# Attention and two feed-forward layers on one core: seven block products in place of eight for three groups of down products of the first layer, three streamed blocks a pair, and first tiles' up products in two parts

## The chip, the cores and the metric

One core of a Trainium2 chip runs the whole program. The metric is the device time of one launch in microseconds, as the median of the runs. The engines are named as the profile names them: PE (TensorE matmul; PEld is its weight load), DVE (VectorE), ACT (ScalarE), POOL (GpSimd) and SP (SyncE, which here only issues transfers).

## The reference

Windowed attention, then a gated feed-forward layer (FFN1), then a second feed-forward layer (FFN2), on 2304 tokens of width 512, all in fp32.

```python
def reference(q, k, v, moe_*, moe2_*):
    attn = softmax(mask(q @ k.T / 8)) @ v            # 4 batches, 8 heads, 576 positions, width 64;
                                                     # each position sees at most 32 others
    x = attn.transpose(0, 2, 1, 3).reshape(2304, 512)
    g = x @ w_gate                                   # 512 -> 1536
    x = (silu(g) * (x @ w_val)) @ w_out              # 1536 -> 512
    h = x @ w_in                                     # 512 -> 2048
    return (h - tanh(h)) @ w_out2                    # 2048 -> 512
```

## The kernel before

**Numbers.** Every operand of a large product is kept as two float32r parts, a high and a low one, and a product of two operands is three matmuls (high·high, high·low, low·high; `PASSES`). The high part is made by a copy on ACT, the low part by a subtraction on DVE (`split_w`, `split_x`, `split_y`). Weights come as 64-bit words and are turned into fp32 on ACT and DVE (`convert`).

**Tiles.** The 2304 tokens are six tiles of 384 (`TT`). The hidden width is cut in blocks of 128, twelve in FFN1 (`k` = 0 to 11). The outer loop of FFN1 goes over groups of hidden blocks, `GROUPS1 = [1, 1, 2, 2, 2, 2, 2]`, so that groups begin at k = 0, 1, 2, 4, 6, 8 and 10. Inside a group the kernel goes over three pairs of tiles (`PAIRS`). For each it makes the *up* products (x times a gate and a value block, tile by tile of 384 columns), then the gating (`times_gate`, `times_val`: Silu on ACT, a multiplication on DVE), the split in two parts (`split_y`), and the *down* products (`ffn1_out`: w_out times y). The down results of a group are copied from PSUM to an `acc` buffer and added to sums in DRAM: the first group stores them (SP), later groups issue an accumulating transfer on POOL (`sum<-acc`), and the last group (k = 10) adds them on chip.

**Seven for eight.** From k = 2 on (`JOIN`), a group has two hidden blocks and a pair has two tiles, and each up product of 2 x 2 blocks (two hidden blocks, two tiles, two halves of the contraction) is made by seven block products (Strassen's scheme in Winograd's form) in place of eight: `seven_up`. It needs sums of weight blocks (`sums_w`) and sums of x blocks (`sums_x`): seven x blocks for each pair (B11, B21, B22, T1 to T4). Three PSUM banks carry a running value: ACT copies a bank's content into the next one (`seed`, the order names it `ps<-ps`), ACT keeps one (`keep`), and two additions on DVE end it. Of the seven x blocks, five stay in SBUF; the other two (T3 and T4) are stored to DRAM when they are made (`spill`, `part<-x`) and loaded again for each pair and group (`parts_of`, `x<-part`), unless the pair before in the program was the same one.

**Order.** Nothing runs in the order in which it is written: every piece of work is a task for a planner (`Plan`) with an engine, a duration, a priority (small first; `when` is a clock of PE work), what it depends on, and the buffers that it needs from rings of fixed sizes (`SLOTS`: 8 PSUM banks `ps`, 4 `acc`, 6 `y`, 6 `t`, 12 + 6 `x`, 10 + 1 `wc`). The planner plays the tasks through once while the program is built. What comes out is a fixed list of instructions for each engine, and each engine runs its list strictly in turn. SP's list holds the transfers of weights (`st<-w`), of attention's inputs (`q`, `v`) and of x blocks. The attention is mixed with the first up products in the first 130 us: its tasks make x piece by piece, heads 0 to 3 in the first of a tile's two x buffers and heads 4 to 7 in the second. A plain up product (`plain_up`, 12 matmuls) waits until both are complete.

## Time and profile before

| | |
|---|---|
| median of 3 runs | 894.3 us (893.83 to 896.32) |
| the profiled execution's own time | 895.31 us |
| its span, first to last instruction | 893.3 us |
| PE, PEld, DVE, ACT, POOL busy in the span | 98%, 93%, 74%, 63%, 11% |
| mean DMA rate | 214 GB/s |

Busy time is the union of an engine's instructions; PE's matmuls overlap, so that their starts tell its rate and not their lengths. A share over the whole span mixes stages: attention with the first groups to about 130 us, FFN1 to about 520 us, FFN2 to the end.

### The profile page before, as it was taken

The numbers are of one execution on the slowest core, as the hardware profiler recorded it, in microseconds if no ns is written. First come the engines' busy times: TensorE is split into PE (matmuls) and PEld (weight loads), VectorE is DVE, ScalarE is ACT, GpSimd is POOL, SyncE is SP. The second block draws the span as 40 slices with busy tenths as digits, with TensorE's granted clock in tenths as the row PEclk, the third lists the DMA queues.
The fourth block names the chain that finished last, engine by engine and source line by source line (L and its number), as shares of the span: only waits on it lengthen the run. The fifth ranks groups of instructions, "written<-read, shape, count | busy, mean of one in ns | idle before, by whom it ended". The sixth has DMA issues, their size and how long they took to land.

```text
span 893.3 us, 15217 instructions
## 1 busy us (share of the span) xinstructions
PE 878.7 (98%) x5310; PEld 829.5 (93%) x5310; DVE 657.6 (74%) x1577; ACT 565.8 (63%) x1467; POOL 94.3 (11%) x122
## 2 busy tenths in 40 slices
PE   7999999999999999999999999999999999999997
PEld 5899999999999999999999998898989989898995
DVE  6899989975645645644757999988887778765575
ACT  6798866756556655655656787765666656555431
POOL 2332220000000000000000000011110111110100
PEclk9899999999999999999999999999999999999999
DMA  9998736996775775686782568889988896968995
GB/s 281 288 293 263 241 114 157 325 299 136 197 184 106 200 189 107 179 210 142 215 266 89 222 227 314 247 211 273 230 212 210 203 252 162 232 127 209 250 286 211
DMA packets 48518, 191.17 MB, mean 214 GB/s; under 512 B 5552, under 2 KB 10672, under 8 KB 48432
## 3 DMA queue, kind: packets, MB, share of 16 engines
q1 hardware_dynamic: 38928, 138.20, 45.2%
q0 software_dynamic: 9504, 51.91, 31.6%
q8 instruction: 44, 0.72, 0.3%
q14 instruction: 42, 0.34, 0.1%
HBM read 114.59 MB, written 75.50 MB: 213 GB/s over the span
## 4 chain that ended last, share of the span: by engine, by line
PE 93%; DVE 3%; DMA 2%; ACT 1%; issue 0%; POOL 0%; SPq 0%; POOLq 0%
PE ps L467 44%; PE ps L667 22%; PE ps L647 16%; PE ps L455 5%; PE ps L371 2%; PE ps L425 2%; DMA q<-qk 2%; PE ps L396 1%; DVE x L439 1%; ACT e L382 1%; DMA mask<-masks 1%; DVE e L376 0%; DVE wc L278 0%; DVE u L301 0%; POOL e L390 0%
## 5 line engine op out<-in xcount | busy, mean ns | idle before, releaser
L467 PE MATMUL ps<-x,wc 128*128 128x384 f32 x2268 | 417.1, 337 | 0.0
L467 PEld LDWEIGHTS ps<-x,wc 128*128 128x128 f32 x2268 | 398.8, 188 | 5.2 <-issue 0.3
L667 PE MATMUL ps<-wc,y 128*128 128x512 f32 (+1 forms) x870 | 208.2, 391 | 0.9 <-DVE t L579 0.9
L612 ACT ACTIVATE acc<-ps 128x384 f32<-128x384 f32 (+1 forms) x246 | 127.4, 528 | 106.3 <-PE ps L667 55.4
L667 PEld LDWEIGHTS ps<-wc,y 128*128 128x128 f32 x870 | 161.8, 188 | 32.6 <-DVE t L579 1.3
L647 PE MATMUL ps<-y,wc 128*128 128x384 f32 x864 | 164.5, 337 | 0.0
L647 PEld LDWEIGHTS ps<-y,wc 128*128 128x128 f32 x864 | 150.9, 188 | 0.5 <-DVE acc L608 0.2
L633 POOL DMA_DIRECT2D sum<-acc x66 | 58.4, 884 | 667.5 <-ACT acc L612 308.4
L531 ACT ACTIVATE y<-t 128x384 fp32r<-128x384 f32 x168 | 86.8, 519 | 37.1 <-DVE t L560 25.1
L534 DVE TENSOR_TENSOR y<-t,y 128x384 fp32r<-128x384 f32 x168 | 92.3, 554 | 10.7 <-ACT y L531 9.9
L278 DVE TENSOR_TENSOR wc<-u,wc 128x512 fp32r<-128x512 f32 x104 | 70.7, 693 | 31.5 <-ACT wc L275 30.9
L275 ACT ACTIVATE wc<-u 128x512 fp32r<-128x512 f32 x104 | 64.9, 630 | 35.8 <-PE ps L467 19.7
L560 DVE SCALAR_TENSOR_TENSOR t<-t,ps 128x384 f32<-128x384 f32 x57 | 31.4, 552 | 64.0 <-PE ps L467 37.3
L478 ACT ACTIVATE ps<-ps 128x384 f32<-128x384 f32 x108 | 51.4, 477 | 26.8 <-PE ps L467 25.3
L576 DVE SCALAR_TENSOR_TENSOR t<-t 128x384 f32<-128x384 f32 x96 | 52.9, 555 | 13.3 <-ACT t L573 13.0
L507 DVE TENSOR_TENSOR ps<-ps,t 128x384 f32<-128x384 f32 x54 | 30.6, 566 | 39.2 <-PE ps L467 38.7
L382 ACT ACTIVATE e<-e,nm 128x96 f32<-128x96 f32 x144 | 52.0, 367 | 10.2 <-DVE nm L376 10.0
L573 ACT ACTIVATE t<-ps 128x384 f32<-128x384 f32 x72 | 35.0, 486 | 30.5 <-DVE ps L507 18.6
L455 PE MATMUL ps<-x,wc 128*128 128x384 f32 x288 | 53.5, 338 | 0.0
L455 PEld LDWEIGHTS ps<-x,wc 128*128 128x128 f32 x288 | 49.6, 188 | 0.2
L293 ACT ACTIVATE u<-st 128x512 f32<-128x512 f32 x68 | 45.1, 666 | 6.3 <-DVE wc L278 5.1
L301 DVE SCALAR_TENSOR_TENSOR u<-st,u 128x512 uint32<-128x512 uint32 x68 | 47.4, 697 | 0.8
(61 smaller groups left out, 795.4 us busy)
## 6 DMA issues: line engine op xcount, KB each, us to landing
sum<-acc POOLq DMA_DIRECT2D x66, 768.0 KB, 7.9
x<-part SPq DMA_DIRECT2D x60, 768.0 KB, 6.8
st<-w SPq DMA_DIRECT2D x68, 512.0 KB, 5.6
q<-qk SPq DMA_DIRECT2D x48, 304.0 KB, 6.8
sum<-acc SPq DMA_DIRECT2D x12, 768.0 KB, 5.8
part<-x SPq DMA_DIRECT2D x12, 768.0 KB, 4.4
acc<-sum SPq DMA_DIRECT2D x12, 768.0 KB, 8.1
v<-vt SPq DMA_DIRECT2D x48, 144.0 KB, 6.5
```

The costliest lines, as they stand in the source:

```text
L275: nc.scalar.activation(out=w()[:, 0, :], in_=u(), func=AF.Copy)
L278: nc.vector.tensor_tensor(out=w()[:, 1, :], in0=u(), in1=w()[:, 0, :].bitcast(F32), op=ALU.subtract)
L382: nc.scalar.activation(out=e()[:, i, :], in_=e()[:, i, :], func=AF.Exp, scale=-1.0, bias=nm()[:, i:i + 1], accum_out=sm()[:, i:i + 1])
L455: nc.tensor.matmul(ps()[:, :TT], lhsT=w()[:, a, kc * P:(kc + 1) * P], rhs=xt[kc // 2]()[:, bb, kc % 2, :], start=(n == 0), stop=(n == 3 * ...
L467: nc.tensor.matmul(ps()[:, :TT], lhsT=w()[:, i, c:c + P], rhs=b()[:, j, k, :], start=(start and n == 0), stop=(n == 5), skip_group_check=True)
L531: nc.scalar.activation(out=y()[:, 0, :], in_=s(), func=AF.Copy)
L534: nc.vector.tensor_tensor(out=y()[:, 1, :], in0=s(), in1=y()[:, 0, :].bitcast(F32), op=ALU.subtract)
L576: nc.vector.scalar_tensor_tensor(out=sq(), in0=sq(), scalar=E0 / E1, in1=sq(), op0=ALU.add, op1=ALU.mult)
L612: nc.scalar.activation(out=o, in_=ps()[:, :c1 - c0], func=AF.Copy)
L633: nc.gpsimd.dma_start(out=keep, in_=at(), accum_op=ALU.add)
L647: nc.tensor.matmul(ps()[:, :TT], lhsT=w[2][0]()[:, a, m * P:(m + 1) * P], rhs=y[0]()[:, bb, :], start=(start and n == 0), stop=(n == 3 * l ...
L667: nc.tensor.matmul(ps()[:, :c1 - c0], lhsT=y[0]()[:, a, s * P:(s + 1) * P], rhs=w[1][0]()[:, bb, c0:c1], start=(n == 0), stop=(n == 3 * le ...
```

## The change

1. In the groups k = 4, 6 and 8 (`SEVEN_DOWN`, all three pairs) the down products of two hidden blocks and two tiles are also made by seven block products for eight (`seven_out`, called in place of `ffn1_out`). They need sums of w_out blocks (`sums_out`, in two buffers `wm`), sums of the gated values (`sums_y`: four subtractions on DVE, and three splits more, in three buffers `ym`), and the seeding between PSUM banks that `seven_up` has.
2. While a pair's x blocks come from the attention (FFN1), four of the seven stay in SBUF and three (T2, T3, T4) go to DRAM and are loaded again. The first use at k = 2 takes them from the buffers in which they were made, without a load. For pair 1 these buffers are of a ring of their own (`xt`), whose room goes to `ym` and `wm` after k = 2 and then, after the last of them, to three more `x` buffers. FFN2 keeps five and streams two, as before.
3. For tiles 0 and 1 in the first group (`APART`), an up product is two tasks of six matmuls. The first needs only heads 0 to 3.

```diff
+Y_SOON, DELAY_7D = 30.0, 9.0
+APART = {(1, 0, 0), (1, 0, 1)}
...
-SLOTS = {"ps": (8, 0), "x": (2 * NT, 6), "acc": (4, 0), "wc": (10, 1), "y": (6, 0), "t": (6, 0), "st": (2, 0), "u": (4, 0), 
+SLOTS = {"ps": (8,), "x": (2 * NT, 3, 0, 0, 3), "xt": (0, 0, 3), "acc": (4,), "wc": (10, 1), "y": (6,), "t": (6,), "st": (2,), "u": (4,),
...
+         "q": (6,), "v": (7,), "e": (6,), "at": (4,), "nm": (8,), "sm": (8,), "ym": (0, 0, 0, 3), "wm": (0, 0, 0, 2)}
+HOMES = ("main", "late", "first", "mid", "last")
+SEVEN_DOWN = {(k, p) for k in (4, 6, 8) for p in range(3)}
...
+    def sums_out(c1, c2, prio):
...
+            tt(out=u2()[:, hi], in0=u1()[:, hi], in1=u2()[:, hi], op=ALU.add)
+            tt(out=u1()[:, hi], in0=u1()[:, lo], in1=u1()[:, hi], op=ALU.subtract)
+            tt(out=u1()[:, lo], in0=u2()[:, hi], in1=u1()[:, lo], op=ALU.subtract)
+            tt(out=u2()[:, lo], in0=u2()[:, lo], in1=u1()[:, lo], op=ALU.subtract)
+
+        a = plan.add("DVE", 1.2, prio, combine, [d1, d2], [u1, u2], port=True)
+        return split_w(u1, [a], prio, new_wm()), split_w(u2, [a], prio, new_wm())
...
-            a = plan.add("PE", MM * 12, prio, lambda wb=wb, ps=ps, xt=x[t]: up(wb, xt, ps), x_done[t] + [done],
-                         [wb, ps] + x[t])
+            ps, a = new_ps(), None
+            for chunks in ((range(KC // 2), range(KC // 2, KC)) if apart else (range(KC),)):
+                need = [d for h in range(2) if KC // 2 * h in chunks for d in x_done[t][h]]
+                a = plan.add("PE", MM * 3 * len(chunks), prio,
+                             lambda wb=wb, ps=ps, xt=x[t], chunks=chunks: up(wb, xt, ps, chunks), need + [done, a],
+                             [wb, ps] + x[t])
...
+    def sums_y(s11, s12, s21, s22, prio):
+
+        b11, b22, b21 = (split_y(*s, prio) for s in (s11, s22, s21))
...
+        t1 = step(s11, s12, s11, [b11[1], s12[1]])
+        y1 = split_y(s11[0], t1, prio, new_ym())
+        t3 = step(s12, s22, s12, [t1, s22[1]])
+        t2 = step(s22, s22, s11, [t3, b22[1]])
+        y2 = split_y(s22[0], t2, prio, new_ym())
+        y3 = split_y(s12[0], t3, prio, new_ym())
+        t4 = step(s21, s21, s22, [t2, b21[1]])
+        return b11, b21, b22, y1, y2, y3, split_y(s21[0], t4, prio)
...
+    def seven_out(ws, sums_o, blocks, tiles, prio):
...
+        for lo, hi in ((0, 2), (1, 3)):
+            pa, pb, pe, e = new_ps(), new_ps(), new_ps(), new_t()
...
+            p1 = pe_task(pa, wa, lo, B11, True, [], [pb, pe])
+            p5 = pe_task(pe, w41, hi, T1, True, [], [pa, pb])
+            sb = plan.add("ACT", 0.39, soon, sow(pb, pa), [p1], [pa, pb], lat=QUICK)
+            ke = plan.add("ACT", 0.39, soon, keep, [p5], [pe, e], lat=QUICK)
+            c11 = pe_task(pa, wb, lo, B21, False, [sb])
+            p6 = pe_task(pb, w23, lo, T2, False, [sb])
+            sc = plan.add("ACT", 0.39, soon, sow(pe, pb), [p6, ke], [pb, pe], lat=QUICK)
+            p3 = pe_task(pb, w41, lo, B22, False, [sc])
+            p7 = pe_task(pe, w23, hi, T3, False, [sc])
+            puts[0].append(plan.add("ACT", 0.39, prio, copy(at1, pa, lo), [c11], [pa, at1]))
+            puts[1].append(plan.add("DVE", 0.48, soon, add(at2, pb, lo), [p3, ke], [pb, e, at2], lat=QUICK))
+            c22 = plan.add("DVE", 0.48, soon, add(at2, pe, hi), [p7, ke], [pe, e, at2], lat=QUICK)
+            puts[1].append(c22)
+            c21 = pe_task(pe, wb, hi, T4, False, [c22])
+            puts[0].append(plan.add("ACT", 0.39, prio, copy(at1, pe, hi), [c21], [pe, at1]))
...
-    def spill(p, parts, prio):
-
-        seven_x[p], spilled[p] = parts[:5], []
-        for o, done in parts[5:]:
+    def spill(p, parts, kept, prio):
+
+        seven_x[p], spilled[p] = parts[:kept], []
+        for o, done in parts[kept:]:
...
+        if p in fresh:
+            fresh.remove(p)
+        elif not again or p not in fetched_x:
...
+                streamed.append(plan.add("NONE", 0.0, prio, lambda: None, [begun] + streamed[-1:], [o]))
+                fetched_x[p].append((o, plan.add("DMA", ISSUE, prio, load, [done, streamed[-1]], [o], lat=SLACK, work=2.15)))
...
+                    if p in down7:
+                        blocks = sums_y(ys[tiles[0]][0], ys[tiles[1]][0], ys[tiles[0]][1], ys[tiles[1]][1], when + 0.02 - Y_SOON)
+                        seven_out(ws, sums_o, blocks, tiles, when + DELAY_7D)
```

The built programs show where the planner now puts the work. Over the whole program PE has 54 matmuls of 384 columns fewer (down products in FFN1: 864 before; 432 plain and 378 in sevens now). DVE has 36 subtractions of `sums_y`, 27 splits into `ym`, 36 additions into `acc`, 12 sums of 256 columns and 6 splits of 512 columns more. ACT has 36 seeds, 18 keeps, 27 splits into `ym` and 6 into `wm` more, and 36 copies into `acc` fewer. SP has 3 stores and 3 loads of x blocks more.

**First place, PE near the start.** The rows of PE before, from the scores of one attention unit (`ps<-q`) on; transposes are `ps<-ident,e`, mixing `ps<-at,v`. `x_276` holds heads 0 to 3 of tile 0, `x_390` heads 4 to 7; `wc_471` and `wc_557` are the gate and value weights of block 0.

```order
L371 MATMUL ps_484<-q_281 128x96 x3
L396 MATMUL ps_508<-ident,e_422 96x128 x3
L371 MATMUL ps_518<-q_329 128x96 x3
L396 MATMUL ps_529<-ident,e_451 96x128 x3
L425 MATMUL ps_540<-at_473,v_270 64x64 x6
L425 MATMUL ps_540<-at_522,v_320 64x64 x6
L371 MATMUL ps_564<-q_363 128x96 x3
L371 MATMUL ps_582<-q_416 128x96 x3
L396 MATMUL ps_606<-ident,e_513 96x128 x3
L371 MATMUL ps_613<-q_438 128x96 x3
L455 MATMUL ps_630<-x_276,wc_471 128x384 x6
L455 MATMUL ps_630<-x_390,wc_471 128x384 x6
```

The same place with the change; everything ahead of it on PE and DVE stands as before.

```order
L395 MATMUL ps_484<-q_281 128x96 x3
L479 MATMUL ps_507<-x_276,wc_471 128x384 x6
L420 MATMUL ps_522<-ident,e_422 96x128 x3
L420 MATMUL ps_530<-ident,e_451 96x128 x3
L395 MATMUL ps_541<-q_329 128x96 x3
L395 MATMUL ps_549<-q_363 128x96 x3
L449 MATMUL ps_566<-at_473,v_270 64x64 x6
L449 MATMUL ps_566<-at_547,v_320 64x64 x6
L395 MATMUL ps_592<-q_416 128x96 x3
L420 MATMUL ps_604<-ident,e_516 96x128 x3
L395 MATMUL ps_610<-q_438 128x96 x3
L479 MATMUL ps_628<-x_276,wc_557 128x384 x6
```

Six matmuls of the first up product stand right behind the scores of `q_281`, ten rows earlier than before, and six of the value product take the place of the second half.

**Second place, PE in the group k = 4.** Before, one tile's down products: four PSUM banks, six matmuls each, in one piece.

```order
L647 MATMUL ps_3607<-y_3462,wc_3330 128x384 x3
L647 MATMUL ps_3607<-y_3577,wc_3558 128x384 x3
L647 MATMUL ps_3619<-y_3462,wc_3330 128x384 x3
L647 MATMUL ps_3619<-y_3577,wc_3558 128x384 x3
L647 MATMUL ps_3630<-y_3462,wc_3330 128x384 x3
L647 MATMUL ps_3630<-y_3577,wc_3558 128x384 x3
L647 MATMUL ps_3638<-y_3462,wc_3330 128x384 x3
L647 MATMUL ps_3638<-y_3577,wc_3558 128x384 x3
```

With the change, a part of a pair's down products (`y`, `ym` against `wc`, `wm`), three matmuls to a block product, between up products (`x`). `ps_4173`, `ps_4186` and `ps_4195` are the three banks of one half; the products into them wait for a seed (ACT) or an addition (DVE) in between.

```order
L490 MATMUL ps_4173<-y_3944,wc_3328 128x384 x3
L490 MATMUL ps_4119<-x_394,wc_3971 128x384 x6
L490 MATMUL ps_4110<-x_3708,wc_3979 128x384 x6
L490 MATMUL ps_4195<-ym_4007,wm_3629 128x384 x3
L490 MATMUL ps_4173<-y_4036,wc_3562 128x384 x3
L490 MATMUL ps_4186<-ym_4082,wm_3618 128x384 x3
L490 MATMUL ps_4214<-y_3944,wc_3328 128x384 x3
L490 MATMUL ps_4110<-x_3749,wc_3884 128x384 x6
L490 MATMUL ps_4186<-y_4033,wm_3629 128x384 x3
L490 MATMUL ps_4195<-ym_4072,wm_3618 128x384 x3
L490 MATMUL ps_4243<-ym_4007,wm_3629 128x384 x3
L490 MATMUL ps_4214<-y_4036,wc_3562 128x384 x3
```

Between the first product into `ps_4173` and the second stand 15 other matmuls; between the two into `ps_4186` stand 9.

**Third place, SP in the groups k = 4 and 6.** Before, each switch of pair loads two x blocks, mixed with weight loads.

```order
L710 DMA x_3391<-part 128x1536
L290 DMA st_3401<-w 128x512
L290 DMA st_3492<-w 128x512
L710 DMA x_3521<-part 128x1536
L290 DMA st_3542<-w 128x512
L710 DMA x_3616<-part 128x1536
L290 DMA st_3626<-w 128x512
L710 DMA x_3736<-part 128x1536
```

With the change, each loads three (`x_3481`, `x_3517`, `x_3552` for one pair, `x_3662`, `x_3708`, `x_3749` for the next).

```order
L298 DMA st_3397<-w 128x512
L814 DMA x_3481<-part 128x1536
L298 DMA st_3490<-w 128x512
L814 DMA x_3517<-part 128x1536
L814 DMA x_3552<-part 128x1536
L814 DMA x_3662<-part 128x1536
L298 DMA st_3692<-w 128x512
L814 DMA x_3708<-part 128x1536
L298 DMA st_3734<-w 128x512
L814 DMA x_3749<-part 128x1536
```

Three buffers take the streamed blocks in turn, so a block's load can start when PE has read the block of the pair before for the last time. Counted in PE's list between that last read and the first read of the new block, over the 21 loads from k = 4 to the first pair of k = 10, there stand 72 to 93 matmuls; before the change at least 114.

## Rows read from the trace of the kernel before

**Rows 1.** The page: busy time of the engines, and the chain that ended last by engine.

```profile
span 893.3 us, 15217 instructions
PE 878.7 (98%) x5310; PEld 829.5 (93%) x5310; DVE 657.6 (74%) x1577; ACT 565.8 (63%) x1467; POOL 94.3 (11%) x122
PE 93%; DVE 3%; DMA 2%; ACT 1%; issue 0%; POOL 0%; SPq 0%; POOLq 0%
```

**Rows 2.** Stretches: length, busy us (instructions) of each engine, clock, DMA share, GB/s.

```profile
247.00:316.00 69.00, 69.00 (x398) 69.00 (x397) 37.41 (x72) 40.20 (x83) 5.47 (x6) 1.00 0.65 160
316.00:385.00 69.00, 69.00 (x398) 69.00 (x397) 37.40 (x72) 40.33 (x83) 5.51 (x6) 1.00 0.64 161
480.00:560.00 80.00, 79.07 (x424) 74.80 (x424) 78.40 (x136) 63.67 (x135) 0.00 (x0) 1.00 0.59 219
140.00:200.00 60.00, 60.00 (x345) 59.68 (x344) 54.96 (x86) 42.09 (x85) 5.19 (x6) 1.00 0.87 264
```

**Rows 3.** The chain that ended last, in a middle group: start us, us, what.

```profile
363.22 4.16 PE ps L467 x24
367.38 4.16 PE ps L647 x24
```

**Rows 4.** Lines, 247 to 454 us: busy us, mean ns of one, idle before.

```profile
L534 DVE TENSOR_TENSOR y<-t,y 128x384 fp32r<-128x384 f32 x36 | 19.6, 552 | 0.4
L507 DVE TENSOR_TENSOR ps<-ps,t 128x384 f32<-128x384 f32 x18 | 10.2, 564 | 14.7 <-PE ps L467 14.5
L324 DVE TENSOR_TENSOR u<-u 128x256 f32<-128x256 f32 x6 | 2.5, 423 | 0.1
L278 DVE TENSOR_TENSOR wc<-u,wc 128x512 fp32r<-128x512 f32 x30 | 20.2, 689 | 19.4 <-ACT wc L275 19.3
L531 ACT ACTIVATE y<-t 128x384 fp32r<-128x384 f32 x37 | 19.2, 519 | 15.0 <-DVE t L560 15.0
L478 ACT ACTIVATE ps<-ps 128x384 f32<-128x384 f32 x36 | 17.1, 476 | 12.0 <-PE ps L467 11.5
L612 ACT ACTIVATE acc<-ps 128x384 f32<-128x384 f32 x72 | 35.2, 489 | 30.9 <-PE ps L647 30.5
L275 ACT ACTIVATE wc<-u 128x512 fp32r<-128x512 f32 x30 | 18.6, 630 | 8.6 <-PE ps L467 6.4 <-PE ps L647 2.0
```

**Rows 5.** Shorter stretches, columns as in the second group.

```profile
280.00:300.00 20.00, 20.00 (x116) 20.00 (x115) 17.13 (x34) 14.57 (x30) 1.78 (x2) 1.00 0.48 95
300.00:320.00 20.00, 20.00 (x117) 20.00 (x116) 10.69 (x21) 11.56 (x25) 1.71 (x2) 1.00 0.83 257
```

**Rows 6.** PE, start of the program: start us, us, instructions [idle before, releaser].

```profile
26.67 0.88 PE L371 MATMUL ps<-q 128*128 128x96 f32 x6 [0.67 <-DMA q<-qk]
27.39 0.49 PE L396 MATMUL ps<-ident,e 128*96 128x128 f32 x3
29.01 1.36 PE L371 MATMUL ps<-q 128*128 128x96 f32 x6 [1.13 <-DVE nm L376]
```

**Rows 7.** Stretches at the start, columns as in the second group.

```profile
20.00:30.00 10.00, 6.73 (x66) 5.57 (x65) 9.83 (x52) 7.42 (x39) 2.89 (x4) 0.96 1.06 287
30.00:40.00 10.00, 10.00 (x90) 9.18 (x90) 7.82 (x49) 8.10 (x41) 2.94 (x4) 0.70 1.05 309
```

**Rows 8.** DVE at the start: the weights' low part, and two waits for PE.

```profile
26.09 1.16 DVE L278 TENSOR_TENSOR wc<-u,wc 128x512 fp32r<-128x512 f32 x1
31.05 0.55 DVE L400 COPY at<-ps 96x384 f32<-96x384 f32 x1 [0.80 <-PE ps L396]
34.16 0.26 DVE L376 CUSTOM_DVE_ANT_0 e<-ps,mask 128x96 f32<-128x96 f32 x1 [1.17 <-PE ps L371]
```

**Rows 9.** Transfers of x blocks, issue to landing, 240 to 460 us.

```profile
L710 SPq DMA_DIRECT2D x<-part x16: 319/327/992, 244.1 to 459.1; - x16
DMA to landing us min/median/max: 4.0/5.4/8.6
```

**Rows 10.** The same, 150 to 240 us.

```profile
DMA to landing us min/median/max: 5.0/8.3/12.8
```

**Rows 11.** SP's waits: us in total, times, longest.

```profile
SPq L290 <- DVE u L306: 346.1, 54, 23.3
```

More of the change, by code (lines that the diff above doesn't have):

```diff
@@ L229, in attention_then_two_ffns @@
     att = att_stack.enter_context(tc.tile_pool(name="att", bufs=1, side="right"))
-    late = []
-    plan = Plan({r: n for r, (n, _) in SLOTS.items()})
+    stacks, later = {h: ctx.enter_context(ExitStack()) for h in HOMES}, {}
+    plan = Plan({r: n[0] for r, n in SLOTS.items()})
     def ring(name, shape, dtype):
@@ L240, in make @@
             else:
-                pool = main if slot < SLOTS[name][0] else late[0]
+                home = next(h for h in range(5) if slot < sum(SLOTS[name][:h + 1]))
+                pool = later[HOMES[home]] if home else main
             return pool.tile(shape, dtype, tag=f"{name}{slot}", name=f"{name}{slot}")
@@ L499, in pe_task @@
             d = {id(wa): da, id(wb): db, id(w24): d24, id(w31): d31}[id(a[0])]
-            return plan.add("PE", MM * 6, prio, lambda: product(ps, a, b[0], start), list(deps) + [d, b[1]],
+            cols = [(2 * a[1] + k) * P for k in range(2)]
+            return plan.add("PE", MM * 6, prio, lambda: product(ps, a[0], cols, b[0], start), list(deps) + [d, b[1]],
                             [ps, a[0], b[0]] + list(more), lat=QUICK)
@@ L554, in times_gate, with times_val @@
         return s, plan.add("DVE", 0.47, prio, mul, [a], [g, s])
-    def times_val(sg, v, prio, scale):
+    def times_val(sg, v, prio, scale, raw):
         (s, a), (v, b) = sg, v
@@ L627, in add_up, with add_store @@
             return at, puts
+        add_store(layer, t, at, puts, first, prio)
+    def add_store(layer, t, at, puts, first, prio):
+        keep = sums[layer - 1][t]
         def store():
@@ L698, in spill @@
         fetched_x.pop(p, None)
+        if kept == 4:
+            fetched_x[p] = parts[kept:]
+            fresh.add(p)
     homes = []
     def parts_of(p, again, prio, begun):
-        if not again or p not in fetched_x:
+        if p in fresh:
+            fresh.remove(p)
+        elif not again or p not in fetched_x:
             fetched_x[p] = []
@@ L794, in attention_then_two_ffns, with given, users, move @@
             fronts = []
-    def leave():
-        att_stack.close()
-        late.append(ctx.enter_context(tc.tile_pool(name="late", bufs=1, side="right", reuse_waits="tile")))
-    left = plan.add("NONE", 0.0, 0.0, leave, att_tasks,
-             gives={r: list(range(a, a + b)) for r, (a, b) in SLOTS.items() if b})
+    def given(*homes):
+        got = {}
+        for h in homes:
+            h = HOMES.index(h)
+            for r, n in SLOTS.items():
+                if n[h:h + 1] not in ((), (0,)):
+                    got.setdefault(r, []).extend(range(sum(n[:h]), sum(n[:h + 1])))
+        return got
+    def users(*rings):
+        return [t for t in plan.tasks if any(b.ring in rings for b in t.bufs)]
+    def move(old, *new):
+        def leave():
+            old.close()
+            for h in new:
+                later[h] = stacks[h].enter_context(tc.tile_pool(name=h, bufs=1, side="right", reuse_waits="tile"))
+        return leave
+    left = plan.add("NONE", 0.0, 0.0, move(att_stack, "late", "first"), att_tasks, gives=given("late", "first"))
     sums = [nc.dram_tensor(f"sum{layer}", (NT, P, KC * TT), F32).ap() for layer in (1, 2)]
     after = {}
-    def finish(layer, h, prio):
+    def finish(layer, h, prio, raw=False):
         if layer == 1:
@@ L836, in attention_then_two_ffns @@
                     extra[c] = sums_w(ws[0][c], ws[1][c], lead + 6 + 2 * c)
+            down7 = [p for p in sevens if layer == 1 and (k, p) in SEVEN_DOWN]
+            if down7:
+                sums_o = sums_out(ws[0][2], ws[1][2], lead + 12)
             if layer == 1:
@@ L854, in attention_then_two_ffns @@
                     for i, t in [(0, tiles[0]), (0, tiles[1]), (1, tiles[1]), (1, tiles[0])]:
-                        ys[t][i] = finish(layer, res[i, t], when + 0.02)
+                        ys[t][i] = finish(layer, res[i, t], when + 0.02 - (Y_SOON if p in down7 else 0.0), p in down7)
+                    if layer == 1 and k == JOIN[p] and p == 1:
+                        plan.add("NONE", 0.0, 0.0, move(stacks["first"], "mid"), users("xt"), gives=given("mid"))
                     begun = q[0][0][1]
@@ L858, in attention_then_two_ffns @@
                     now_early = ys[tiles[0]][0][1]
+                    if p in down7:
+                        blocks = sums_y(ys[tiles[0]][0], ys[tiles[1]][0], ys[tiles[0]][1], ys[tiles[1]][1], when + 0.02 - Y_SOON)
+                        seven_out(ws, sums_o, blocks, tiles, when + DELAY_7D)
+                        when += 7.3
+                        if k == max(SEVEN_DOWN)[0] and not any((k, o) in SEVEN_DOWN for o in order[order.index(p) + 1:]):
+                            plan.add("NONE", 0.0, 0.0, move(stacks["mid"], "last"), users("ym", "wm"), gives=given("last"))
+                        before = (layer, p)
+                        continue
                     turns = tiles[::-1] if ends else tiles
```

94 lines of the change are left out of this document (61 added, 33 removed).

## The prediction

> **What bounds the kernel now.** I read the page first, then the chain, then stretches. Over the span PE is busy 98%, and the chain that ended last lies on PE for 93% of its length, on DVE for 3% and on DMA for 2% [rows 1]. Busy time alone would not prove much, since PE's matmuls overlap, but the starts do: in a middle group 24 matmuls of 384 columns take 4.16 us on the chain, for up and for down products alike, so 0.1733 us each [rows 3]. A group of FFN1 with two blocks has 3 pairs x (84 up + 48 down) = 396 matmuls, which is 68.6 us at that rate, and two neighbouring groups show 398 starts in 69.00 us without a gap [rows 2]. In these groups PE waits for nobody. DVE is busy 37.4 of 69 us and ACT 40.2 [rows 2], so both have room. The kernel therefore loses time on PE only near the start, where PE stands still for inputs [rows 6] and its clock falls to 0.70 of full speed in the mean over 30 to 40 us [rows 7], and a little around 540 us, where DVE is busy 78.4 of 80 us and PE is short of 0.93 us [rows 2]. So work taken off PE in the middle is time taken off the end, as long as DVE, ACT and the transfers still deliver.
>
> **The change, part by part.**
>
> *Sevens in the down products.* A pair's down products were 2 tiles x 4 banks x 6 = 48 matmuls; they become 2 halves x 7 x 3 = 42. Over three groups and three pairs that is 9 x 6 = 54 matmuls fewer; 54 x 0.1733 = **-9.4 us** on PE [rows 3].
>
> *What it costs elsewhere.* DVE gets 99 instructions of 384 columns more (36 subtractions, 27 splits, 36 additions), at 0.552 to 0.564 us [rows 4], say 0.555: 54.9 us; 12 sums of 256 columns at 0.423: 5.1; 6 splits of 512 at 0.689: 4.1 [rows 4]. Together 64.1 us, 21.4 for each group. A group shrinks to 69.0 - 18 x 0.1733 = 65.9 us, and DVE's load in it rises from 37.4 to 58.8 us, 89%. ACT gets 36 seeds at 0.476, 18 keeps and minus 36 copies at 0.489, 27 splits at 0.519 and 6 at 0.630 [rows 4]: 17.1 - 8.8 + 14.0 + 3.8 = 26.1 us, 8.7 a group, 48.9 of 65.9 us or 74%. Both are hidden under PE's matmuls, and the question is whether 89% on DVE stays hidden. The trace has two stretches to measure by: at 92% (140 to 200 us) PE is busy all 60.00 us; at 98% (480 to 560 us) it lacks 0.93 us in 80 [rows 2]. The lower bound is 0. At the rate of the second, three groups (198 us) would lose 198 x 0.93 / 80 = 2.3 us. As 89% is nearer to the first, I take **+0.7 us**.
>
> The load is not even. In 280 to 300 us DVE has 17.1 us of work because the weights of the next group are converted there, and in the next 20 us 10.7 [rows 5]. With 21.4 x 20 / 65.9 = 6.5 us more, the first becomes 23.6 in 20 and the second 17.2: DVE falls 3.6 us behind and gets 2.8 back. The gated values can bear that: in PE's list at least 90 matmuls (15.6 us) stand between the last up product of a pair and the first block product that reads a value made from it. The additions inside the sevens can bear less: a block product that continues a bank stands as little as 9 matmuls (1.6 us) behind the one that DVE's addition or ACT's seed waits for. The up products have lived with 6 (1.0 us) to a seed and 12 (2.1 us) to an addition. An addition alone takes 0.56 us, so 1.6 us leaves room for one instruction of 512 columns ahead of it on DVE (0.69) but not for two. Should every microsecond of the backlog fall on such an addition, each group loses 3.6 us: that is the upper bound for a rival below, 10.8 us.
>
> *Three streamed blocks.* Per switch of pair SP now loads three x blocks, not two, into three buffers without a spare. The room between the last read of a buffer and the first read of its new block was at least 114 matmuls (19.8 us) and is now 72 to 93 (12.5 to 16.1 us). From issue to landing a load took 5.4 us in the median and 8.6 at most in this part of the program [rows 9], and up to 12.8 in the busier stretch from 150 to 240 us [rows 10]. So the median load has 7 us to spare, the slowest seen 4, and I cost this at nothing; without that cover each microsecond past 12.5 would stop PE's up products, at each of the seven switches that these 21 loads serve. SP issues in order, and its longest total wait is a weight load that needs DVE to have emptied its buffer: 346 us in 54 waits [rows 11]. Some x loads stand right behind such a weight load, so a late DVE would delay them too. At k = 2 the blocks are used where they were made: three more stores, six loads fewer. DVE's work there is the same, and so I cost it at nothing as well; what would cover a late split there is a DVE at 92% beside a PE without a gap [rows 2].
>
> *First tiles in two parts.* Up to the scores at 26.67 us, PE's list is unchanged. Then it ran a transpose at 27.39 and stood idle 1.13 us until 29.01 [rows 6]. Now six matmuls of the first up product stand there; their last input, the low part of `wc_471`, is written on DVE from 26.09 to 27.25 [rows 8], so they can start at 27.4 and take 1.04 us. What follows on PE is attention, which DVE has to keep up with. Below, the gain is bounded by nothing (the six merely fill a hole, and the six that now stand a little later run while the clock is low). Above, it is the 1.04 us plus what the low clock cost: 0.70 in 30 to 40 us and 0.96 in 20 to 30 [rows 7] make (0.30 + 0.04) x 10 = 3.4 us, together 4.4. In the same stretch DVE waited for PE only 0.80 + 1.17 = 1.97 us [rows 8]; by that much the chain of attention can move forward before DVE sets its pace. I take **-2.0 us**.
>
> On the clock, the rows show the granted level at half (1.2 of 2.4 GHz) after a stretch in which PE was busy 6.73 of 10 us [rows 7]. The Trainium skill, "TensorE: Matmul & The Clock Gate", Part 1, states that the lower level is the default and that activity releases it; this trace agrees that the fall follows the sparse stretch, and by that rule alone, with six matmuls put into the hole, the fall might not come at all and the gain would be the upper bound above.
>
> *Sum.* The profiled execution took 895.3 us, 1.0 above the median of the three runs. 895.3 - 9.4 + 0.7 - 2.0 = 884.6, and 883.6 on the scale of the median.
>
> **The rivals.**
>
> *Nothing lost, clock kept.* The start gains all 4.4, DVE loses nothing in the middle, and the 0.93 us around 540 us goes as well: 895.3 - 9.4 - 4.4 - 0.9 = 880.6, as median 879.6. For it speaks that the extra six matmuls lie right in the sparse stretch; against it that DVE is busy 9.83 of 10 us just before [rows 7].
>
> *Nothing at the start, the measured rate in the middle.* The clock falls as before and the twelve matmuls only change places; the middle loses 2.3: 895.3 - 9.4 + 2.3 = 888.2, as median 887.2. For it: PE's list up to 26.67 us is unchanged, and with it what the clock has seen until then.
>
> *DVE becomes the bound.* The backlog falls on the additions: up to 10.8 us lost, half of it a milder case. With nothing won at the start: 891.3 to 896.7, as median 890.3 to 895.7. For it: the 23.6 us of work in 20. Against it: PE lost nothing beside a DVE at 92%.
>
> *Streamed blocks come late: slower than before.* If a load needs longer than 12.5 us, PE waits at each of seven switches. To give back 9.4 + 2.0 - 0.7 and end 0.3% (2.7 us) above 894.3, each must wait (10.7 + 2.7) / 7 = 1.9 us, so landings from 14.4 us on decide; at 15, 7 x 2.5 = 17.5 us makes it 901. Against it: 8.6 us was the most here, and 12.8 anywhere before FFN2 [rows 9, 10]; for it: weight loads ahead of x loads on SP, whose waits for DVE reach 23.3 us [rows 11].
>
> That the change does nothing is excluded, since the 54 matmuls are gone from PE's list.
>
> **How the numbers follow.** The forecast (881 to 887) gets 0.48; nothing lost and the clock kept (879.5 to 881) 0.14; nothing won at the start (885 to 889) 0.18; DVE as the bound (889 to 896) 0.13; late blocks (above 896) 0.07. The likeliest gives 883.6. The range from 879.5 to 890.5 leaves out the upper half of the fourth case, the fifth and a little below, under 2 in 10. A measurement of this kernel can tell about 0.3% (2.7 us) from no change: faster is below 891.6. The first three cases and part of the fourth, less some doubt about a static list under a fuller DVE, make 0.83; between 891.6 and 897.0 lies 0.10; above, 0.07.
>
> **What would show it.** Right: in the three groups PE without idle time, each 66 us and 378 matmuls long, DVE near 59 us busy in each; PE's waits for DVE and ACT in the block products under 2.3 us in all; landings of x blocks below 12.5 us; the granted clock above 0.70 in 30 to 40 us and the attention's chain some 2 us earlier at 40 us. Wrong: idle time of PE ahead of block products with `y` or `ym` that ends with DVE's additions (the third rival), or ahead of up products that ends with a landing of `x<-part` (the fourth); PE ahead at 40 us but not at 200 us, so that the gain of the start is lost again to a DVE that is busy throughout; or new idle time around the end of FFN1, where three x buffers come free only after the last `ym` and `wm`.

## The result, and the profile after

The changed kernel took 884.07 us in the median of 4 runs (880.9 to 886.3), the kernel before, on the same chip, 894.26 us (4 runs, 893.83 to 896.32): ratio 0.988, 95% interval 0.984 to 0.992. The profiled execution of the changed kernel is its fastest run, 880.9 us with a span of 879.1; it lies 3.2 us below the median, and why is a question of the start (below).

The page of the changed kernel: span, busy time, and the chain that ended last.

```profile
span 879.1 us, 15303 instructions
PE 866.4 (99%) x5256; PEld 817.9 (93%) x5256; DVE 711.1 (81%) x1694; ACT 582.9 (66%) x1518; POOL 93.0 (11%) x122
PE 95%; DVE 3%; ACT 1%; issue 0%; POOL 0%; POOLq 0%; DVEq 0%
```

Against [rows 1] PE has 54 matmuls fewer, DVE is busy 53.5 us longer, and the chain still lies on PE. Stretches of the changed kernel, in the columns of [rows 2]: its three groups, the two stretches of [rows 5], the end of FFN1, and the start.

```profile
243.70:309.70 66.00, 66.00 (x380) 66.00 (x379) 57.50 (x116) 47.32 (x102) 4.40 (x5) 1.00 0.71 191
309.70:375.70 66.00, 66.00 (x380) 66.00 (x379) 55.95 (x112) 46.65 (x100) 5.26 (x6) 1.00 0.71 192
375.70:441.70 66.00, 66.00 (x380) 66.00 (x379) 55.90 (x110) 46.68 (x101) 5.24 (x6) 1.00 0.84 237
280.00:300.00 20.00, 20.00 (x117) 20.00 (x116) 17.89 (x36) 14.62 (x32) 1.78 (x2) 1.00 0.64 144
300.00:320.00 20.00, 20.00 (x116) 20.00 (x115) 17.62 (x36) 13.67 (x30) 1.73 (x2) 1.00 0.71 211
480.00:560.00 80.00, 80.00 (x416) 73.62 (x415) 79.62 (x147) 63.02 (x138) 0.00 (x0) 1.00 0.68 250
20.00:30.00 10.00, 8.75 (x88) 7.44 (x90) 9.77 (x53) 7.25 (x38) 2.89 (x4) 1.00 1.05 304
30.00:40.00 10.00, 9.55 (x106) 8.46 (x102) 8.81 (x55) 9.38 (x48) 3.55 (x5) 1.00 1.04 317
```

A group now has 66 us, and PE is busy in all of it. DVE is busy 55.9 to 57.5 us in a group where it had 37.4. Around 540 us the 0.93 us of [rows 2] are gone. In 20 to 40 us the clock stays at 1.00, where [rows 7] had 0.96 and 0.70. PE's waits for the streamed blocks would show in the chain of waits; it runs through all three groups on PE's products alone. Behind it stand the landings of x blocks, first of the 25 loads in 240 to 460 us, which answer to [rows 9], then of the 21 in 225 to 420 us:

```profile
243.71 198.56 PE ps L490 x1137
```

```profile
DMA to landing us min/median/max: 4.2/6.2/15.0
```

```profile
DMA to landing us min/median/max: 4.2/5.2/8.0
```

The 21 loads, as many as the prediction counted, stay under its 12.5 us. Those above 8.0 us were issued from 420 us on, for the last group, whose buffers come free with the sevens' end; the last three exceed 12.5 us, but no product waited for one.

The place of the up products in two parts, on PE, against [rows 6]:

```profile
25.36 0.88 PE L395 MATMUL ps<-q 128*128 128x96 f32 x6 [0.23 <-DMA q<-qk]
26.02 0.60 PE L479 MATMUL ps<-x,wc 128*128 128x384 f32 x2
26.77 0.97 PE L479 MATMUL ps<-x,wc 128*128 128x384 f32 x4 [0.16 <-DVE wc L286]
27.58 0.85 PE L420 MATMUL ps<-ident,e 128*96 128x128 f32 x6
```

The six products stand right behind the scores, and the hole of 1.13 us is filled.

**Where the time came from.** One row splits an execution in two: the first and the last start of the block products that read x (line 467 before, 490 after). Line and form, count, ns of one (least, median, most), first and last start. First the kernel before, then the changed one.

```profile
L467 PE MATMUL ps<-x,wc x2268: 331/336/444, 159.8 to 875.0; 128*128 128x384 f32 x189
```

```profile
L490 PE MATMUL ps<-x,wc x2232: 331/334/443, 155.7 to 860.6; 128*128 128x384 f32 x186
```

Up to the first such product the changed kernel is 4.1 us earlier (155.7 against 159.8); from the first to the last it needs 704.9 us instead of 715.2, 10.3 less. The 54 matmuls make 9.4 of these; the wait of 0.93 us near 540 us, which is gone, accounts for the rest. The start's 4.1 us belong to this execution only, as the next run shows.

### The profile page after: what moved, and what is told of

It reads as the page before. It is cut to its first block, busy times and chain, and to the rows that moved or that the text cites. A ratio compares the mean times of both kernels' runs of the same rounds, so it can differ in the third digit from the quotient of the medians.

```text
span 879.1 us, 15303 instructions
## 1 busy us (share of the span) xinstructions
PE 866.4 (99%) x5256; PEld 817.9 (93%) x5256; DVE 711.1 (81%) x1694; ACT 582.9 (66%) x1518; POOL 93.0 (11%) x122
## 4 chain that ended last, share of the span: by engine, by line
PE 95%; DVE 3%; ACT 1%; issue 0%; POOL 0%; POOLq 0%; DVEq 0%
PE ps L490 53%; PE ps L766 23%; PE ps L746 8%; PE ps L479 5%; PE ps L395 2%; PE ps L449 2%; PE ps L420 2%; DVE e L400 1%; DVE x L463 1%; PE ps L885 1%; DVE at L424 0%; ACT e L406 0%; DVE wc L286 0%; DVE sm L410 0%; DVE u L309 0%
## 5 line engine op out<-in xcount | busy, mean ns | idle before, releaser
L490 PEld LDWEIGHTS ps<-x,wc 128*128 128x128 f32 x2232 | 392.5, 188 | 5.6 <-DVE t L626 0.2
L659 ACT ACTIVATE acc<-ps 128x512 f32<-128x512 f32 (+1 forms) x174 | 92.5, 542 | 71.7 <-PE ps L766 51.0
L501 ACT ACTIVATE ps<-ps 128x384 f32<-128x384 f32 x144 | 67.9, 475 | 23.6 <-PE ps L490 21.4
L746 PE MATMUL ps<-y,wc 128*128 128x384 f32 x432 | 82.4, 337 | 0.0
L746 PEld LDWEIGHTS ps<-y,wc 128*128 128x128 f32 x432 | 75.1, 188 | 0.3 <-ACT acc L659 0.2
L623 DVE SCALAR_TENSOR_TENSOR t<-t 128x384 f32<-128x384 f32 x96 | 52.8, 553 | 10.8 <-ACT t L620 10.2
L620 ACT ACTIVATE t<-ps 128x384 f32<-128x384 f32 x72 | 34.9, 485 | 26.6 <-DVE ps L534 17.6
L479 PEld LDWEIGHTS ps<-x,wc 128*128 128x128 f32 x288 | 49.6, 188 | 0.5 <-DVE wc L286 0.5
L309 DVE SCALAR_TENSOR_TENSOR u<-st,u 128x512 uint32<-128x512 uint32 x68 | 47.3, 695 | 0.9
L314 DVE SCALAR_TENSOR_TENSOR u<-st,u 128x512 uint32<-128x512 uint32 x68 | 46.7, 686 | 0.3
```

The lines of the kernel that those rows point to most:

```text
L479: nc.tensor.matmul(ps()[:, :TT], lhsT=w()[:, a, kc * P:(kc + 1) * P], rhs=xt[kc // 2]()[:, bb, kc % 2, :], start=(n == 0), stop=(n == 3 * ...
L490: nc.tensor.matmul(ps()[:, :TT], lhsT=w()[:, i, c:c + P], rhs=rhs, start=(start and n == 0), stop=(n == 3 * len(cols) - 1), skip_group_che ...
L501: nc.scalar.activation(out=ps()[:, :TT], in_=src()[:, :TT], func=AF.Copy)
L623: nc.vector.scalar_tensor_tensor(out=sq(), in0=sq(), scalar=E0 / E1, in1=sq(), op0=ALU.add, op1=ALU.mult)
L659: nc.scalar.activation(out=o, in_=ps()[:, :c1 - c0], func=AF.Copy)
L746: nc.tensor.matmul(ps()[:, :TT], lhsT=w[2][0]()[:, a, m * P:(m + 1) * P], rhs=y[0]()[:, bb, :], start=(start and n == 0), stop=(n == 3 * l ...
```

## The experiments

Times are medians; each ratio is to the kernel before on the same chip in the same series, with its 95% interval. Three series, in which the kernel before took 895.46, 894.93 and 895.34 us.

**The changed kernel again.**

> The changed kernel again, unaltered, to see more of its runs: the first ones fell into two bunches, 881 to 882 and 886 us. Theory (the gain has three parts: 54 matmuls fewer, about -9.4 us; the start, -0 to -4.4 us, by whether TensorE's clock falls between 20 and 40 us; the wait near 540 us, -0.9 us): the bunches differ in the start alone; a run near 881 us shows a mean granted clock of 0.998 or more, one near 886 us a lower one, and median runs lie at 882 to 886 us, ratio 0.985 to 0.991. Rival (the bunches come from the middle, where VectorE sometimes falls behind): spans differ by 4 to 5 us at the same mean clock.

884.25 us, ratio 0.987 (0.985 to 0.989). Its profiled execution took 886.3 us. The same row of it:

```profile
L490 PE MATMUL ps<-x,wc x2232: 331/334/440, 160.5 to 865.8; 128*128 128x384 f32 x186
```

From first to last 705.3 us, as before (704.9); but the first product starts at 160.5 instead of 155.7 us. So 4.8 of the 5.4 us between these two executions of one program arise in the start. PE in that start, and two stretches:

```profile
20.49 0.53 PE L420 MATMUL ps<-ident,e 128*96 128x128 f32 x3
24.41 1.59 PE L395 MATMUL ps<-q 128*128 128x96 f32 x6 [3.38 <-DMA q<-qk]
```

```profile
20.00:30.00 10.00, 6.62 (x53) 6.09 (x51) 7.01 (x38) 5.78 (x27) 1.73 (x3) 0.66 0.98 275
30.00:40.00 10.00, 9.52 (x124) 8.77 (x121) 8.76 (x53) 7.23 (x38) 2.49 (x4) 1.00 1.02 321
```

A transfer of q came late, PE stood still for 3.38 us ahead of the edited place, and the granted clock fell to half: scores that took 0.88 us in the other execution took 1.59. The theory holds in where the two executions differ. The wait for the transfer comes first, and the low clock goes with it; how much of the 4.8 us each of them makes isn't separated here.

**Without the up products in two parts.**

```
-APART = {(1, 0, 0), (1, 0, 1)}
+APART = set()
```

> The change without the up products in two parts: the start's instructions as before the change. Theory: the 9.4 us of the sevens and the 0.9 us near 540 us stay, the start's gain goes: 894.3 - 9.4 - 0.9 = 884.0 us, in the middle no wait of TensorE, and a low clock in 30 to 40 us as before. Rival 1 (the sevens lose 2.3 us or more in the middle and the start gave more than 2 us): 886.5 us or more. Rival 2 (the start gives nothing that lasts): the same time as the changed kernel on this chip, within 1 us.

885.20 us, ratio 0.988 (0.986 to 0.990); the four runs took 884.0 to 888.4. Against the changed kernel's 884.25 the two parts give about 1 us, less than two sets of four runs can tell, so theory (884.0) and second rival (within 1 us) both fit. In its profiled execution the granted clock was 0.83 in 20 to 30 us and 1.00 in 30 to 40, so it was not low where it was expected to be. The profiled execution is the slowest of the four and has a wait of its own, far from the edit; PE's wait in 560 to 600 us, and what ACT did before it:

```profile
PE ps L490 <- DVE t L537: 2.0, 1, 2.0
```

```profile
581.76 0.66 ACT L301 ACTIVATE u<-st 128x512 f32<-128x512 f32 x1 [4.34 <-DMA st<-w]
```

A weight of FFN2 landed 14.6 us after its issue (the load in its place 10.3 and 10.2 us in the changed kernel's two profiled executions), ACT and with it DVE stood behind it, and PE ran dry. The other three runs of this program have no profile, so whether they wait there too isn't known.

**Without the sevens in the down products.**

```
-SEVEN_DOWN = {(k, p) for k in (4, 6, 8) for p in range(3)}
+SEVEN_DOWN = set()
```

The slots change with it: none for ym and wm, and x has (2 * NT, 3, 0, 3).

> The change without the sevens in the down products (eight block products as before, no buffers for their sums): what is left is the up products in two parts and three streamed blocks a pair. Theory: only the start's gain is left, 0 to -4.4 us: 890 to 894.3, most likely 892 us, 378 matmuls a group of FFN1 back to 396. Rival (most of the gain is the start's or the streaming's, and the sevens give little): 888 us or less.

894.59 us, ratio 0.999 (0.998 to 1.001), 12 runs. Without the sevens nearly nothing is left of the gain: the theory's side, 0.3 us past its upper end.

**Only the streamed blocks.** Both edits above together.

> Only the three streamed blocks a pair (and their three buffers) are left of the change; neither the sevens in the down products nor the up products in two parts. Theory: a streamed block lands within its cover, so nothing changes: 894.3 us within 1 us, no wait of TensorE for a DMA in the middle. Rival 1 (late blocks): TensorE waits before up products, 895.5 us or more. Rival 2 (using the blocks of the first group where they were made helps): 893 us or less.

896.64 us, ratio 1.001 (0.999 to 1.003), 12 runs. Against the run before it, which differs only in the two parts, 2.0 us more: so the two parts give 2.0 us here. Its row:

```profile
L490 PE MATMUL ps<-x,wc x2232: 331/336/445, 159.8 to 877.3; 128*128 128x384 f32 x186
```

The first product starts when it did before the change (159.8), but from first to last it needs 717.5 us, 2.3 more than before. Neither theory nor rival said where: not in FFN1's groups, but in two places where PE waits for a gated value. PE's waits in 480 to 640 us, the products behind each, and ACT's waits for weights in 560 to 610:

```profile
PE ps L766 <- DVE t L626: 2.8, 2, 1.6
```

```profile
544.29 1.63 PE L766 MATMUL ps<-wc,y 128*128 128x512 f32 x6 [1.19 <-DVE t L626]
607.38 3.02 PE L766 MATMUL ps<-wc,y 128*128 128x512 f32 x12 [1.64 <-DVE t L626]
```

```profile
ACT u L301 <- DMA st<-w: 6.8, 3, 3.0
```

The first is the wait near 540 us that the kernel before has too, with 0.93 us. Only the second, 1.64 us in FFN2, is new: there DVE waits for ACT and ACT for weights. The profiled execution without sevens has the same two waits (1.2 and 1.6 us), the changed kernel's two have neither. The planner orders SP's loads ahead of the second place otherwise here; that this order is the cause was not tried. In the medians the streamed blocks alone cost 1.2 us (896.64 against 895.46), which the interval doesn't tell from nothing.

**Dummy products in the start, before and after the change.**

```
         def scores():
...
+            scored.append(1)
+            if 7 <= len(scored) <= 16:
+                for _ in range(5):
+                    nc.tensor.matmul(ps()[:, 288:], lhsT=warm[:, :P], rhs=warm[:, 288:], start=True, stop=True)
```

> The kernel before the change, with 5 dummy bf16 products of 224 columns on TensorE ahead of each of the 7th to the 16th scores (50 in all, about 4.7 us at the full clock, into unused columns of the scores' bank; the result doesn't change). They stand where TensorE waits for q between 14 and 35 us. Theory (what the start can give is the clock's: a late q leaves TensorE idle, and the clock falls behind it): the granted clock stays at 1.00 in 20 to 40 us, 2 to 3 us faster than the kernel before, and runs that agree more closely than before's 893 to 899 us. Rival (the start is set by the transfers and VectorE, and a low clock there costs nothing): the same time within 1 us, or slower where the dummies delay the scores.

894.76 us, ratio 1.000 (0.999 to 1.002), 12 runs: the same as before. Its start, against [rows 7]:

```profile
20.00:30.00 10.00, 8.20 (x91) 7.49 (x90) 9.43 (x46) 7.03 (x36) 2.89 (x4) 1.00 1.06 283
30.00:40.00 10.00, 10.00 (x117) 9.43 (x115) 9.67 (x56) 9.62 (x46) 3.87 (x5) 1.00 1.05 304
```

The clock did stay at 1.00, and nothing was won. The time is the rival's; its reason, that a low clock costs nothing there, isn't shown, since the dummies may cost as much as the clock gave back.

> The changed kernel with the same 50 dummy products ahead of the 7th to the 16th scores. Theory: the clock stays up and runs lie at 880.5 to 882.5 us, like the faster half of the changed kernel's runs (880.9 to 886.3 so far). Rival 1 (clock has no part in it): runs spread as before, median 884. Rival 2 (the dummies delay the scores by up to 4.7 us, and attention with them): 886 to 889 us.

883.50 us, ratio 0.988 (0.986 to 0.990); five runs from 882.9 to 884.6, closer together than the changed kernel's, but in the median not faster by more than the noise: the first rival's median, without its spread.

**More work for DVE.** All additions inside the sevens twice:

```
-                return lambda: nc.vector.tensor_tensor(out=at()[:, m * TT:(m + 1) * TT], in0=ps()[:, :TT], in1=e(), op=ALU.add)
+                def one():
+                    for _ in range(2):
+                        nc.vector.tensor_tensor(out=at()[:, m * TT:(m + 1) * TT], in0=ps()[:, :TT], in1=e(), op=ALU.add)
+                return one
```

> The changed kernel with each of the 36 additions of VectorE inside the sevens of the down products issued twice (the second writes the same again; the result doesn't change): 36 x 0.556 = 20 us more of VectorE, 6.7 us a group, and each product that waits for an addition gets its release 0.56 us later. Profile of the changed kernel: VectorE 170 us busy of the 200 from 240 to 440 us, 56 of 66 a group; 63 of 66 with this. Theory (the covers of the sevens have room: the prediction's middle term of 0.7 us is really about 0): 0 to +2 us against the changed kernel (884). Rival (the 9 matmuls, 1.6 us, of cover are nearly used up by backlog, so VectorE is about to become the bound): +5 us or more, TensorE idle ahead of block products that wait for VectorE's addition.

894.85 us, ratio 1.000 (0.999 to 1.002): the whole gain is gone, the rival's side. DVE and PE around 318 us, and PE's waits in 240 to 460 us:

```profile
317.25 2.20 DVE L714 TENSOR_TENSOR acc<-ps,t 128x384 f32<-128x384 f32 x4
```

```profile
319.51 0.79 PE L490 MATMUL ps<-y,wc 128*128 128x384 f32 x3 [1.63 <-DVE acc L714]
```

```profile
PE ps L490 <- DVE acc L714: 7.8, 12, 1.6
```

Two additions of one half stand one behind the other on DVE, so the last ends two durations later. In 243.7 to 441.7 us DVE was busy 176.5 of 198 us, 89%: in the mean its share is not full, and yet PE waits 12 times. Summed over the starts of PE's products between 240 and 460 us, the time beyond 0.174 us each is 12.5 us here, 0.7 in the changed kernel and 0.5 in the one before.

**The same amount elsewhere on DVE.** Four of the seven low splits of y twice:

```
-        y1 = split_y(s11[0], t1, prio, new_ym())
+        y1 = split_y(s11[0], t1, prio, new_ym(), 2)
```

So also y2, y3 and the last of the seven; with the 2, `split_y` issues the low split twice.

> The changed kernel with the low split of each y that is made from a sum (4 of the 7 of each pair in the sevens of the down products) issued twice on VectorE: again 36 x 0.555 = 20 us more in the three groups, as much as doubling all additions brought, but at values that are read by TensorE many products later (the result doesn't change). Theory (what costs is the place: TensorE waits where an addition inside a seven ends late, whatever VectorE's share): 0 to +3 us against the changed kernel (884), few waits, as an instruction more in the queue can still delay an addition behind it. Rival (VectorE's total load costs): the same 894 to 895 us as with the additions doubled.

892.60 us, ratio 0.997 (0.995 to 0.998): 8 to 9 us given back, nearer to the rival. My theory that only the place counts falls. PE's waits in 240 to 460 us:

```profile
PE ps L490 <- DVE t L537: 2.3, 3, 1.1
PE ps L490 <- DVE acc L713: 0.9, 2, 0.5
PE ps L490 <- ACT ps L501: 0.5, 1, 0.5
```

The split itself is not waited for here. Five of the six waits are for additions, those inside the up products' sevens (line 537) and those inside the down products': DVE works through its list in order, and a split put anywhere into a full stretch (19.65 of 20 us busy in 280 to 300) makes the additions behind it late. By starts, 8.8 us are lost between 240 and 460 us.

**Only the later addition twice.** As with all additions, but for one of the two of a half (`add` gets a count).

```
-            c22 = plan.add("DVE", 0.48, soon, add(at2, pe, hi), [p7, ke], [pe, e, at2], lat=QUICK)
+            c22 = plan.add("DVE", 0.48, soon, add(at2, pe, hi, 2), [p7, ke], [pe, e, at2], lat=QUICK)
```

> The changed kernel with only the later of the two additions of each half of a seven issued twice (18 x 0.556 = 10 us more of VectorE; the result doesn't change). In the trace of the changed kernel the last block product of a half starts 0.59 to 1.52 us after the end of the addition that it needs, in all 18 places. Theory (the room is these 0.59 us and more): a delay of 0.56 us fits, 0 to +1.5 us against the changed kernel (884). Rival (cost in proportion to VectorE's load): half of what doubling all additions cost, +5 us, 889.

887.13 us, ratio 0.991 (0.988 to 0.993): about 3 us given back, between the two. PE waits twice (0.9 us), and by starts 3.2 us are lost. The room that was worked out is seen in the rerun of the changed kernel, on DVE and PE:

```profile
382.44 1.01 DVE L712 TENSOR_TENSOR acc<-ps,t 128x384 f32<-128x384 f32 x2
```

```profile
384.09 0.69 PE L490 MATMUL ps<-y,wc 128*128 128x384 f32 x3
```

The second addition ends at 383.45, its product starts at 384.09, 0.64 us later. That room holds for one addition that is late by itself, not for what other late instructions add.

**Streamed blocks twice.** In a first attempt the second loads were not in the program.

> The changed kernel with each streamed x block of FFN1's three-block pairs loaded twice into the same buffer, one load behind the other (the result doesn't change): the landing of the second counts, 4.2 us median and 8.0 at most become about 8.5 and up to 16. Theory (the cover is the 72 to 93 products counted, 12.5 to 16.1 us): 0 to +2 us against the changed kernel, TensorE waits for x only where a landing exceeds 12.5 us. Rival (cover nearly used up, or SP's queue delays the weight loads behind them): +5 us or more, idle ahead of up products.

883.50 us, ratio 0.988 (0.986 to 0.990), with as many loads as the changed kernel: four more runs of it, and nothing on the question. The 4.2 us that the expectation calls the median landing are the least; the median is 5.2, the most 8.0, and the next expectation doubles the same figure. Then with the second loads:

```
-                def load(o=o, home=home):
-                    nc.sync.dma_start(out=o().bitcast(F32).rearrange("p s k n -> p (s k n)"), in_=home)
+                def load(o=o, home=home, times=2 if len(spilled[p]) == 3 else 1):
+                    for _ in range(times):
+                        nc.sync.dma_start(out=o().bitcast(F32).rearrange("p s k n -> p (s k n)"), in_=home)
```

> The changed kernel with each streamed x block of FFN1's three-block pairs really loaded twice into the same buffer (in the earlier attempt the second loads weren't in the program: the test read the list of blocks when it had two again). The second load waits for the first, so the landing that counts is 8.5 us in the median and up to 16. Theory (cover of 12.5 to 16.1 us): 0 to +3 us against the changed kernel (884), waits of TensorE for x only where the second landing comes after 12.5 us. Rival (cover nearly used up, or SP's weight loads behind the x loads come late): +5 us or more.

969.20 us, ratio 1.082 (1.080 to 1.084): the rival, and far beyond it. SP's waits for its own loads, then PE's, both in 240 to 460 us:

```profile
SPq L815 <- DMA x<-part: 108.9, 18, 9.2
```

```profile
PE ps L490 <- DMA x<-part: 40.3, 8, 9.3
```

The dose was other than meant. SP issues in order, and each second load holds SP until the first has landed, 6.1 us in the mean; so the three blocks of a switch come one after another, four landings long or some 24 us, and the loads behind them wait too. It shows that the cover is finite and what lies behind it, 5.0 us at each of 8 waits, not how much a load could grow by itself. These waits are not all of the 85 us: in 243.7 to 441.7 us the granted clock was 0.91, where the changed kernel has 1.00, and later waits come on top.

**Two sevens more.**

```
-SEVEN_DOWN = {(k, p) for k in (4, 6, 8) for p in range(3)}
+SEVEN_DOWN = {(k, p) for k in (2, 4, 6, 8) for p in range(3)} - {(2, 0)}
...
-                        plan.add("NONE", 0.0, 0.0, move(stacks["first"], "mid"), users("xt"), gives=given("mid"))
+                        plan.add("NONE", 0.01, 0.0, move(stacks["first"], "mid"), users("xt"), gives=given("mid"))
```

> The changed kernel with two more sevens in the down products, the second and third pair of the group ahead of the three (the sums' buffers come free just then): 12 products fewer on TensorE, 8 additions and the like more for VectorE, which was busy 92% there. Theory (sevens are free as long as each addition ends in time): -2.1 us against the changed kernel, 882. Rival (VectorE, the fuller one there, ends additions late): 884 us or more, TensorE waiting for additions or for y around 225 to 245 us.

892.50 us, ratio 0.997 (0.996 to 0.998): 8 us slower than the changed kernel, with 12 products fewer. Between 200 and 460 us, where the added sevens lie, PE waits for nothing. The loss lies ahead of them, at 146 us. PE's one long wait, and ACT then:

```profile
PE ps L479 <- ACT acc L659: 6.4, 1, 6.4
```

```profile
148.32 0.84 ACT L827 ACTIVATE x<-acc 128x768 fp32r<-128x768 f32 x1 [0.39 <-DVE acc L845]
152.43 3.17 ACT L659 ACTIVATE acc<-ps 128x384 f32<-128x384 f32 x8 [3.26 <-DVE x L830]
```

In this program the planner put the splitting of x earlier into ACT's and DVE's lists; ACT's copies, which empty the banks for PE, stand behind it. That the buffers' other timing is the reason was not tried. In 150 to 160 us the clock is at 0.67 besides. So PE waited nowhere beside the added sevens, and the order that came with them cost more than they gave. No version here beat the changed kernel by more than the noise.

## Why the prediction was right

**The sevens, -9.4 us.** Right, in size and in mechanism: a group went from 69 to 66 us with PE busy throughout. The middle and end became 10.3 us shorter, and by pairs of runs that differ in the sevens (884.25 against 894.59, 885.20 against 896.64) they are worth 10.3 and 11.4 us. What is above 9.4 was not in the sum: the wait near 540 us (0.93 us before, 1.2 without the sevens), which stood with the first rival, and the 1.6 us at 607 us that the two kernels without sevens have.

**Stalls in the middle, +0.7 us.** Too high; it was the lower bound, nothing. DVE's load was estimated at 58.8 us a group and came to 55.9 to 57.5. The instructions were counted rightly, but their times overlap: two additions take 1.01 us together, not 1.10, and over the whole program the durations of DVE's single instructions add up to 61 us more than before, while its busy time rises by 53.5. The fullest stretch did come. Between 280 and 320 us the windows of the profiled execution hold 17.9 and 17.6 us, but they cut the stretch in two; in the rerun, which runs 4.8 us later, they hold

```profile
280.00:300.00 20.00, 20.00 (x116) 20.00 (x115) 19.71 (x41) 16.28 (x34) 1.78 (x2) 1.00 0.61 136
300.00:320.00 20.00, 20.00 (x117) 20.00 (x116) 15.76 (x33) 13.62 (x30) 0.86 (x1) 1.00 0.70 215
```

So DVE was as good as full there, as the prediction had it (23.6 us of work in 20, then 17.2), and PE still waited for nothing; how far behind DVE fell can't be read from a busy share. The step that argued from shares, 92% on DVE beside a PE without a gap, was therefore no measure of the room, and that the stalls came to nothing does not bear it out. With 89% in the mean PE waited 12 times in the run with all additions doubled. The third rival, DVE as the bound, was near: the change's 64 us of DVE work cost nothing, 10 us more (one instruction in each half of a seven) cost 3 and 20 us more (two in each) cost 8 to 11. The cover of 9 matmuls was the right place to look; it left 0.6 to 1.5 us in all 18 places (worked out from the starts in the rerun's trace).

**Streamed blocks, 0.** Right for their place: no product waited for one. That the same edit alone would come with a new wait of 1.6 us at 607 us was not foreseen; in the changed kernel it does not show.

**The start, -2.0 us.** Right in size, with a wide spread: 1.0 and 2.0 us in the two pairs of runs that differ in it. The profiles agree. In the eight profiled executions with the parts and without dummies or added sevens the first block product that reads x starts at 155.7 to 160.5 us, median 157.4; in the three without the parts at 158.9 to 159.8. The 4.1 us of the first profiled execution, close to the upper bound, were a lucky one. The clock's part in that bound (3.4 us) has no support: where dummies held the clock at 1.00, the time stayed, though what the dummies cost isn't known. By the Trainium skill, "TensorE: Matmul & The Clock Gate", Part 1, activity releases the lower level, and the run with dummies agrees (1.00 in 20 to 40 us). That a clock kept up brings the upper bound, this run does not bear out.

**The sum.** 883.6 against 884.07 us, closer than the parts are known, and so in part luck. The forecast's gain of 10.7 us had 0.7 too much for stalls and left out 0.9 near 540 us. With the start at 1.0 to 2.0 the parts as measured make 11.3 to 12.3 us; the changed kernel gained 10.2, 11.2 and 11.4 us in three series (884.07, 884.25 and 883.50 against 894.26, 895.46 and 894.93). Where the rest of up to 2 us stays is open.

## What to carry to other kernels

An engine beside the bound is not free up to 100%: find the instruction on it that the bound engine waits for soonest, and measure the room between its end and the first use; that room, 0.6 to 1.5 us here, and not the 15% of idle time, is what the next edit can spend. Look also for stretches in which the engine is full: its mean of 85% in the three groups hid a stretch of 20 us with 19.7 busy, and there any instruction more, wherever its result is used, makes those behind it late. When a planner writes the order, an edit that frees buffers or moves loads also rewrites lists far from it, so look for new waits over the whole span (at 146 and 607 us here, each far from the products that an edit touched). And compare starts over many runs: one program's start differed by 4.8 us between two executions.

## What the runs showed of the hardware

PE waited 6.1 us for transfers of q in one execution, 3.38 of it at once, and 1.0 us in all in another of the same program; the granted clock was at 0.66 in 20 to 30 us of the first, half speed for two thirds of the stretch, and 1.00 in 20 to 40 us of the second. Holding the clock up with 50 dummy products did not shorten the kernel. Additions of 0.55 us that follow each other on DVE start about 0.47 us apart, so sums of single durations overstate its load (58.8 us a group worked out, 55.9 to 57.5 measured).
